# Attention and GLU on one core: VectorE's exponential as one quadratic with two PV products instead of four shifted patterns, and any score job open to either engine

## Chip, cores, metric

The kernel runs on one core of a Trainium2 chip. The metric is device time in microseconds (us) of one execution, medians over several executions. The engines are PE (TensorE; PEld is its weight loads), ACT (ScalarE), DVE (VectorE), POOL (GpSimd) and SP (which issues DMAs).

## The reference, cut to what matters

```python
xn = layernorm(x)                                   # x: 1 x 2048 x 640, bf16
q, k, v = heads(xn @ wqkv)                          # 32 heads of 20
p = softmax(q @ k.T * 20 ** -0.5)                   # 32 x 2048 x 2048: 134 million exponentials
s = merge(p @ v) @ wo
g = silu((sigmoid(xn @ w_gate) * (xn @ w_up)) @ w_down)      # F = 1728
out = x + s * g
```

## The kernel before

Attention is cut into 32 blocks (8 groups of four heads, times 4 chunks of 512 queries). A block has 64 **score jobs**: one head against one tile of 128 keys, a 128x512 tile of scores in one of the program's banks in PSUM (the memory to which it has PE write its products). There are 2,048 jobs in all. PE makes the scores, ACT or DVE makes the exponential, PE multiplies it with V (the **PV** matmuls, four heads at once in four column strips; in the trace before, a round of four starts 0.222 us after the round before it, at the median) into one accumulator bank; the row sums come from a column of ones in V. A clever part of the program is its issue order: at build time a loop with estimated durations decides, step by step, what each engine does next. It fills the gaps of PE with GLU and projection work.

ACT takes two or three jobs at a time, with its own exponential instruction:

```python
exp_act(pt[:, 2, :], bank[nexp % 2])                 # a third job, if there is one: 128x512
exp_act(pt[:, 0:2, :], scA[nexp % 2])                # two jobs at once: 128x1024
```

DVE approximates. It turns scores into integers that are bf16 bits of a power of two, linear between powers; four such patterns, shifted by a quarter octave each (an octave is a factor of two) and weighted through V itself and three scaled copies of it, average the ripple out:

```python
# one per job: float scores in PSUM -> int16
nc.vector.tensor_scalar(out=d["iv"][:, j, :], in0=bank[bk], scalar1=I_OFF, scalar2=I_LOW, op0=ALU.add, op1=ALU.max)
# four per four jobs (128x2048, int16 -> int16), one for each shift k
nc.vector.tensor_scalar(out=pb[:, k, :, :].bitcast(I16), in0=iv, scalar1=0.25, scalar2=cst, op0=ALU.mult, op1=ALU.add)
# four PV matmuls per job
lhsT = vts[...] if not k else vss[pr % 2][:, DKT.index(kt), k - 1, ...]
```

The scaled copies of V exist only for 4 of the 16 key tiles, so DVE takes those tiles whole (four heads each), 512 jobs at most; what it has not taken by the end of a block goes to ACT. The thresholds of the order loop matter later. The one called SLACK below says how soon DVE must be free for a score matmul to be issued for it; the loop reads it at a second place too, where it decides how long a job waiting for conversion may stand back behind a pass:

```python
NPT, NPB, NIV = (2, 4), 2, 2          # buffers: exp outputs (of 2 and of 3 jobs), pass outputs, converted jobs
# ... cut ...
busy = max(0.0, free["DVE"] - now) + T_IV * len(dq)
if d_can and busy <= T_F + T_MODE + PL + SLACK:      # 0.2133 + 0.107 + 0.21 + SLACK
    d_bank = ...                                     # a free PSUM bank for DVE's job
# ... cut: the second place, in DVE's own part of the loop ...
if iv_ok and not (dve_last == "iv" and pass_ok and now < dq[0][3] + SLACK):
```

Of the kernel before, what the change touches and what calls it, by code (L numbers as in the profile page):

```python
# [20 lines left out]
GH = 4  # L21
# [5 lines left out]
ND = 4  # L27
# [4 lines left out]
URGENT, ROUNDS, HOLD, SLACK, LEAD, LAG, D_LAST, D_LAST_END = 0.1, 4, 0.3, 0.1, 20.0, -5.0, 16, 8  # L32
D_ORD, M_ORD, WAIT3, FALL = 0, 1, 0.0, 1

LOG2E = 1.4426950408889634
UNIT = 512.0
ALPHA = (1.0, 215.0 / 256.0, 181.0 / 256.0, 152.0 / 256.0)
NB = len(ALPHA)
I_OFF = 28672.0
I_LOW = -32700.0  # L40


def _log_shift():
    y = (np.arange(4096) + 0.5) / 4096
    tot = np.zeros_like(y)
    for b, a in enumerate(ALPHA):
        z = y + b / NB
        n = np.floor(z)
        tot += a * 2.0 ** n * (1.0 + z - n)
    return -float(np.log2(np.mean(tot / 2.0 ** y)))  # L50


DELTA = _log_shift()
# [3 lines left out]
def kernel(  # L57
# [47 lines left out]
    xnT = persist.tile([P, KD, S], BF16, name="xnT")  # L105
# [3 lines left out]
    vss = [persist.tile([P, max(ND, 1), NB - 1, 2 * GH, VW], BF16, name=f"vs{i}") for i in range(2)] if ND else None  # L109
# [12 lines left out]
    DKT = [(2 * i + 1) * TT // (2 * ND) for i in range(ND)] if ND else []  # L122
    AKT = [k for k in range(TT) if k not in DKT]

    wqkv_v = A_wqkv.rearrange("(kd p) (t c) -> p kd t c", p=P, t=3)
# [20 lines left out]
    def k_mm(ps, g, c):  # L146
        for kd in range(KD):
            nc.tensor.matmul(ps, lhsT=wslice(g, 1, kd), rhs=xnT[:, kd, c * 512:(c + 1) * 512],
                             start=(kd == 0), stop=(kd == KD - 1))
# [21 lines left out]
    def q_mm(ps, g, c):  # L171
        for kd in range(KD):
            nc.tensor.matmul(ps, lhsT=wslice(g, 0, kd), rhs=xnT[:, kd, c * QC:(c + 1) * QC],
                             start=(kd == 0), stop=(kd == KD - 1))
# [12 lines left out]
    def v_mm(ps, w, tts):  # L187
        for i, tt in enumerate(tts):
            for kd in range(KD):
                nc.tensor.matmul(ps[:, i * 2 * GC:(i + 1) * 2 * GC], lhsT=xnT[:, kd, tt * P:(tt + 1) * P],  # L190
                                 rhs=w[:, kd, :], start=(kd == 0), stop=(kd == KD - 1))

    def v_evac(ps, pr, tts, copy=None):
        copy = copy or nc.vector.tensor_copy
        n = len(tts)
        src = ps[:, 0:n * 2 * GC].rearrange("p (t h e) -> p t h e", t=n, e=DH)
        copy(out=vts[pr % 2][:, tts[0]:tts[0] + n, :, 1:1 + DH], in_=src)
        for i, tt in enumerate(tts):
            if tt in DKT:
                vf = wk.tile([P, 2 * GC], FP32, tag="vf", bufs=1, name="vf")  # L200
                copy(out=vf, in_=ps[:, i * 2 * GC:(i + 1) * 2 * GC])
                for b in range(1, NB):
                    nc.gpsimd.tensor_scalar(out=vss[pr % 2][:, DKT.index(tt), b - 1, :, 1:1 + DH],
                                            in0=vf.rearrange("p (h e) -> p h e", e=DH),
                                            scalar1=ALPHA[b], scalar2=0.0, op0=ALU.mult, op1=ALU.add)
# [4 lines left out]
    with tc.tile_pool(name="ln", bufs=2) as lp, \  # L210
# [17 lines left out]
        def constants():  # L228
# [6 lines left out]
            for b in range(1, NB):  # L235
                nc.gpsimd.memset(vss[0][:, :, b - 1, :, 0:1], ALPHA[b])
            nc.gpsimd.memset(vts[0].rearrange("p t h c -> p (t h) c")[:, :, 0:1], 1.0)

        def more_constants():
# [8 lines left out]
            for b in range(1, NB):  # L248
                nc.gpsimd.memset(vss[1][:, :, b - 1, :, 0:1], ALPHA[b])
# [27 lines left out]
        def scale(c):  # L277
# [7 lines left out]
            for kd in range(KD):  # L285
# [4 lines left out]
                dst = xnT[:, kd, c * 512:(c + 1) * 512]  # L290
# [82 lines left out]
    ob = []  # L373
# [6 lines left out]
    T_IV, T_PASS, T_ON = 0.605, 0.605, 0.60  # L380
    NPT, NPB, NIV = (2, 4), 2, 2
# [44 lines left out]
    def k_mm1(ps, g, c, kd):  # L426
        nc.tensor.matmul(ps, lhsT=wslice(g, 1, kd), rhs=xnT[:, kd, c * 512:(c + 1) * 512],
                         start=(kd == 0), stop=(kd == KD - 1))

    def mk_q(b, at):  # L430
# [6 lines left out]
        def mm(kd):  # L437
            nc.tensor.matmul(st["ps"], lhsT=wslice(g, 0, kd), rhs=xnT[:, kd, c * QC:(c + 1) * QC],
# [23 lines left out]
    def u_mm(st, u, i, c, kd):  # L462
        nc.tensor.matmul(st["ps"][0:UC, :], lhsT=wus[u][:, kd, i, :], rhs=xnT[:, kd, c * QC:(c + 1) * QC],  # L463
# [100 lines left out]
    def mk_v(pr, tts, at):  # L564
# [5 lines left out]
        def mm(i, kd):  # L570
            nc.tensor.matmul(st["ps"][:, i * 2 * GC:(i + 1) * 2 * GC],
                             lhsT=xnT[:, kd, tts[i] * P:(tts[i] + 1) * P],
                             rhs=wvs[pr][:, kd, :], start=(kd == 0), stop=(kd == KD - 1))

        def done(t):
            for tt in tts:
                v_at[(pr, tt)] = t + (2.5 if tt in DKT else 0.0)
        nd = sum(tt in DKT for tt in tts)
        return Item([("PE", alloc, [(0.08, lambda i=i, kd=kd: mm(i, kd)) for i in range(len(tts)) for kd in range(KD)]),
                     ("DVE", 0.065 + 0.167 * len(tts) + 0.231 * nd, lambda: v_evac(st["ps"], pr, tts), "free", done)], at)  # L580

    def mk_gu(c, kf, at):
# [16 lines left out]
        def mm(key, i, kd):  # L599
            w = wgu_tiles[(c, k2)]  # L600
            nc.tensor.matmul(st[key][0:fs, :], lhsT=w[:, i, kd, ko * P:ko * P + fs],  # L601
                             rhs=xnT[:, kd, c * QC:(c + 1) * QC], start=(kd == 0), stop=(kd == KD - 1))
# [9 lines left out]
        def mm2(kd):  # L612
            nc.tensor.matmul(st["g"], lhsT=wgu_tiles[(c, k2)][:, 0, kd, P:2 * P],
                             rhs=xnT[:, kd, c * QC:(c + 1) * QC], start=(kd == 0), stop=(kd == KD - 1))
# [83 lines left out]
    def load_out(tt):  # L698
        if tt in out_tiles:
            return  # L700
        if not ob:
            ob.append(late.tile([P, 14 * D], BF16, name="ob", tag="wd"))
        o2 = ob[0][:, tt % 3 * 4 * D:(tt % 3 + 1) * 4 * D]
        out_tiles[tt] = (o2[:, 0:D], o2[:, 2 * D:4 * D].bitcast(FP32), o2[:, D:2 * D])
# [3 lines left out]
    def mk_out(tt, h, at):  # L708
# [21 lines left out]
        def ev():  # L730
            xr, gqr, ot = out_tiles[tt]
            sl = slice(h * HD, (h + 1) * HD)
            tmp = ob[0][:, 12 * D + h * D:13 * D + h * D].bitcast(FP32)
            nc.vector.scalar_tensor_tensor(out=tmp, in0=st["ps"][:, 0:HD], scalar=0.25,
                                           in1=gqr[:, sl], op0=ALU.mult, op1=ALU.mult)
            nc.gpsimd.tensor_tensor(out=ot[:, sl], in0=tmp, in1=xr[:, sl], op=ALU.add)
            if h == 1:
                nc.sync.dma_start(out=out2[tt * P:(tt + 1) * P, :], in_=ot)
        return Item([("PE", alloc, [(0.136, lambda kd=kd: mm(kd)) for kd in range(KD + split)]),
                     ("DVE", 0.40, ev, "free", mark("o", tt, h))], at, need=(NG - 1) * NQC + tt // 4,  # L740
                    pre=[("d", NQC - 1, t4, i) for t4 in range(4) for i in range(2)] + (
# [39 lines left out]
    a_left = {b: [(kt, j) for kt in AKT for j in range(GH)] for b in range(NBLK)}  # L781
    d_left = {b: list(DKT) for b in range(NBLK)}
# [3 lines left out]
    def base():  # L786
        while head_blk[0] < NBLK - 1 and not a_left[head_blk[0]] and not d_left[head_blk[0]]:
# [3 lines left out]
    def claim_act(n):  # L791
        got = []
        for b in range(base(), NBLK):
            while len(got) < n and (a_left[b] or d_left[b]):
                if q_at.get(b, 1e9) > now:
                    return got
                if not a_left[b]:
                    kt = d_left[b].pop()
                    a_left[b] = [(kt, j) for j in range(GH)]
                kt, j = a_left[b].pop(0)  # L800
                if any(x[2] == j for x in got):
                    a_left[b].insert(0, (kt, j))
                    return got
                got.append((b, kt, j))
                claimed[0] += 1
            if len(got) == n:
# [3 lines left out]
    def claim_dve():  # L810
        for b in range(base(), min(NBLK, base() + 2)):
            if d_left[b] and len(a_left[b]) >= (D_LAST if b < NBLK - 1 else D_LAST_END):
                if q_at.get(b, 1e9) > now:
                    return None
                claimed[0] += GH
                return b, d_left[b].pop(0)
# [15 lines left out]
    def add_unit(b, kt, j, src, k, ready, rel):  # L832
        if k is None or k == NB - 1:
# [13 lines left out]
    def pv_emit(us, end):  # L847
        for u in us:
# [7 lines left out]
            if not k:  # L856
                lhsT = vts[pr % 2][:, kt, go * GH + j, 0:DH + 1]
            else:
                lhsT = vss[pr % 2][:, DKT.index(kt), k - 1, go * GH + j, 0:DH + 1]
# [43 lines left out]
    def passes(iv, pb, k):  # L903
        cst = 128.0 * (127.0 + k / NB + DELTA) - I_OFF / 4.0
        nc.vector.tensor_scalar(out=pb[:, k, :, :].bitcast(I16), in0=iv, scalar1=0.25, scalar2=cst,  # L905
                                op0=ALU.mult, op1=ALU.add)


    xfl = xnT.rearrange("p k s -> p (k s)")
# [4 lines left out]
    def tail_load():  # L914
        for t4 in range(4):
            r = slice(4 * (NQC - 1) * P + t4 * P, 4 * (NQC - 1) * P + (t4 + 1) * P)
            o2 = xfl[:, t4 * 4 * D:(t4 + 1) * 4 * D]
            tail.append((o2[:, 0:D], o2[:, 2 * D:4 * D].bitcast(FP32), o2[:, D:2 * D]))
# [3 lines left out]
    def tail_steps():  # L922
# [36 lines left out]
        for t4 in range(4):  # L959
            xr, gqr, ot = tail[t4]  # L960
            nc.vector.scalar_tensor_tensor(out=tmps[t4], in0=mains[t4], scalar=0.25, in1=gqr[:, 0:512],
                                           op0=ALU.mult, op1=ALU.mult)
            if t4 < 2:
                nc.gpsimd.tensor_tensor(out=ot[:, 0:512], in0=tmps[t4], in1=xr[:, 0:512], op=ALU.add)
        xg = xfl[:, 0:16 * D].rearrange("p (t u) -> p t u", u=4 * D)
# [3 lines left out]
                                       in1=xfl[:, 0:16 * D].bitcast(FP32).rearrange(  # L969
                                           "p (t u) -> p t u", u=2 * D)[:, :, D + 512:2 * D],  # L970
                                       op0=ALU.mult, op1=ALU.mult)
        nc.vector.tensor_tensor(out=xg[:, :, D + 512:2 * D], in0=tmp.rearrange("p (t e) -> p t e", e=EX),
                                in1=xg[:, :, 512:D], op=ALU.add)
        for t4 in (2, 3):
            xr, gqr, ot = tail[t4]
            nc.vector.tensor_tensor(out=ot[:, 0:512], in0=tmps[t4], in1=xr[:, 0:512], op=ALU.add)
        for t4 in range(4):
            r = slice(4 * (NQC - 1) * P + t4 * P, 4 * (NQC - 1) * P + (t4 + 1) * P)
            eng = nc.sync if t4 % 2 == 0 else nc.scalar
            eng.dma_start(out=out2[r, :], in_=tail[t4][2])  # L980

    with tc.manual_schedule(engines={ENG.PE, ENG.Activation, ENG.DVE}):
# [32 lines left out]
        def due():  # L1015
            return total * min(1.0, progress() / (NBLK - NQC - 0.2))
# [18 lines left out]
        while pv_block[0] < NBLK or items or glu_items or any(it.i < len(it.ops) for it in active):  # L1035
# [33 lines left out]
            for eng in ("ACT", "DVE"):  # L1069
# [51 lines left out]
                if iv_ok and not (dve_last == "iv" and pass_ok and now < dq[0][3] + SLACK):  # L1121
                    dve_last = "iv"
                    d, j, bk, _ = dq.pop(0)
                    nc.vector.tensor_scalar(out=d["iv"][:, j, :], in0=bank[bk], scalar1=I_OFF,  # L1124
                                            scalar2=I_LOW, op0=ALU.add, op1=ALU.max)
# [4 lines left out]
                    if d["n"] == GH:  # L1130
                        dve_pass.append(d)
                elif pass_ok:
# [3 lines left out]
                    if k == 0:  # L1136
                        d["pb"] = w2.tile([P, NB, GH, QC], BF16, tag="pb", bufs=NPB, name="pb")
# [170 lines left out]
```

## Time and profile before

Time: 879.36 us (878.77 to 879.71, 3 runs). The profiled execution has a span of 879.2 us.

| stage | us |
|---|---|
| start: layer norm, first projections | 0 to 43 |
| main stage: first to last exp of ACT | 43.0 to 856.8 |
| tail: last normalisation, output product | 856.8 to 879.2 |

The head of the profile page: busy time, share of the span and instructions of each engine, then the granted clock of TensorE (the part of its full speed that the chip let it run at) in 40 equal slices, in tenths, then the chain of work that ended last by engine.

```profile
PE 822.0 (93%) x7176; PEld 297.1 (34%) x7176; DVE 708.5 (81%) x1203; ACT 829.9 (94%) x1098; POOL 100.3 (11%) x142
...
PEclk9999999999999999999999999999999999989999
...
ACT 42%; PE 35%; DVE 13%; issue 8%; DMA 1%; POOL 1%; POOLq 0%; DVEq 0%; ACTq 0%
```

Three stretches of the main stage from the table of stretches (from:to, length, then busy us of each engine with its instruction count, clock, DMA share, GB/s):

```profile
200.00:300.00 100.00, 97.51 (x851) 35.46 (x849) 82.25 (x140) 98.27 (x128) 7.98 (x9) 1.00 0.23 59
300.00:400.00 100.00, 97.23 (x871) 35.22 (x871) 79.28 (x132) 99.50 (x133) 9.15 (x13) 1.00 0.25 68
400.00:500.00 100.00, 98.33 (x870) 33.60 (x867) 92.81 (x157) 99.06 (x126) 6.99 (x7) 1.00 0.21 56
```

ACT has nothing left; DVE has 18, 21 and 7 of 100 us free here. Records of one engine overlap (the next instruction starts before the record of the last one ends), so for costs I use the distance from one start to the next. Here are ACT and then DVE from the timeline (start, duration, engine, what):

```profile
404.39 1.06 ACT L87 ACTIVATE pt_5530<-scA_570 128x1024 bf16<-128x1024 f32 x1
405.29 1.07 ACT L87 ACTIVATE pt_5540<-scA_571 128x1024 bf16<-128x1024 f32 x1
406.20 1.08 ACT L87 ACTIVATE pt_5550<-scA_570 128x1024 bf16<-128x1024 f32 x1
407.10 0.67 ACT L87 ACTIVATE pt_5561<-bk_573 128x512 bf16<-128x512 f32 x1
407.58 1.11 ACT L87 ACTIVATE pt_5561<-scA_571 128x1024 bf16<-128x1024 f32 x1
```

```profile
404.48 0.69 DVE L1124 TENSOR_SCALAR iv<-bk_574 128x512 int16<-128x512 f32 x1
405.08 0.69 DVE L905 TENSOR_SCALAR pb<-iv 128x2048 int16<-128x2048 int16 x1
405.68 0.69 DVE L1124 TENSOR_SCALAR iv<-bk_573 128x512 int16<-128x512 f32 x1
```

A two-job exp occupies ACT for 0.90 us although its record says 1.06 to 1.08 (404.39 to 405.29); a one-job exp 0.48 (407.10 to 407.58). Over the main stage the medians are 0.904 and 0.477. A conversion and a pass occupy DVE 0.60 each. And the groups of instructions (count | busy us, mean ns | idle before them, what ended it):

```profile
L905 DVE TENSOR_SCALAR pb<-iv 128x2048 int16<-128x2048 int16 x412 | 287.9, 723 | 2.7
L1124 DVE TENSOR_SCALAR iv<-bk_574 128x512 int16<-128x512 f32 x147 | 100.6, 685 | 37.9 <-PE bk_574 L820 37.2
L1124 DVE TENSOR_SCALAR iv<-bk_573 128x512 int16<-128x512 f32 x147 | 100.4, 683 | 31.6 <-PE bk_573 L820 31.4
...
L1124 DVE TENSOR_SCALAR iv<-bk_572 128x512 int16<-128x512 f32 x118 | 80.6, 683 | 20.0 <-PE bk_572 L820 19.5
```

Conversions are 147 + 147 + 118 = 412, so DVE did 412 jobs (20%) and ACT 1,636. DVE idled 89 us before conversions, nearly all of it waiting for PE's score matmuls.

### The profile page before, as it was taken

To read this page: it belongs to the slowest core of one execution; us is meant where nothing else is said; L and a number is where in the kernel's file an instruction comes from. 1 tells how busy PE (TensorE), PEld (TensorE's weight loads), DVE (VectorE), ACT (ScalarE), POOL (GpSimd) and SP (SyncE) were. 2 spreads that over 40 slices of the span, in tenths; PEclk is the share of its full clock that TensorE was granted. 3 is DMA by queue.
4 is the path that set the end of the run, shared out by engine and by line. 5 is a ranking of instruction groups with operands and counts; after the bars stand their busy time and mean duration, and the time that the engine had idled before them with its cause. 6 is when DMAs were issued, how large, how long until landed. Compare 5 with 4: busy or idle time off the path is not lost.

```text
span 879.2 us, 18755 instructions
## 1 busy us (share of the span) xinstructions
PE 822.0 (93%) x7176; PEld 297.1 (34%) x7176; DVE 708.5 (81%) x1203; ACT 829.9 (94%) x1098; POOL 100.3 (11%) x142
## 2 busy tenths in 40 slices
PE   2799999999999999999999999999999999987896
PEld 1532333333333333343333333333323333322333
DVE  6568878986789987769999878688688698678984
ACT  4699999999999999999999999999999999999990
POOL 5200000112000000111000000012000000001333
PEclk9999999999999999999999999999999999989999
DMA  7241222222112232211123233211122221321432
GB/s 207 61 123 44 62 63 77 62 55 53 49 52 78 72 81 73 71 44 35 37 57 94 64 74 82 62 45 41 52 73 70 60 61 49 109 82 47 116 111 83
DMA packets 92987, 62.32 MB, mean 71 GB/s; under 512 B 34649, under 2 KB 86409, under 8 KB 92897
## 3 DMA queue, kind: packets, MB, share of 16 engines
q1 hardware_dynamic: 91456, 59.48, 24.9%
q10 hardware_dynamic: 1440, 1.64, 0.6%
q8 instruction: 56, 0.92, 0.5%
q14 instruction: 35, 0.28, 0.1%
HBM read 46.24 MB, written 12.39 MB: 67 GB/s over the span
## 4 chain that ended last, share of the span: by engine, by line
ACT 42%; PE 35%; DVE 13%; issue 8%; DMA 1%; POOL 1%; POOLq 0%; DVEq 0%; ACTq 0%
PE oacc L860 9%; DVE pb L905 5%; PE scA_571 L820 5%; PE scA_570 L820 5%; DVE iv L1124 4%; PE bk_574 L601 4%; ACT tnh L87 2%; PE bk_572 L463 1%; PE bk_574 L639 1%; PE bk_574 L463 1%; PE bk_572 L601 1%; DVE xn L283 1%; PE bk_573 L601 1%; PE bk_573 L639 1%; DMA xt<-in_A_x_dram 1%
## 5 line engine op out<-in xcount | busy, mean ns | idle before, releaser
L905 DVE TENSOR_SCALAR pb<-iv 128x2048 int16<-128x2048 int16 x412 | 287.9, 723 | 2.7
L1124 DVE TENSOR_SCALAR iv<-bk_574 128x512 int16<-128x512 f32 x147 | 100.6, 685 | 37.9 <-PE bk_574 L820 37.2
L1124 DVE TENSOR_SCALAR iv<-bk_573 128x512 int16<-128x512 f32 x147 | 100.4, 683 | 31.6 <-PE bk_573 L820 31.4
L890 POOL TENSOR_TENSOR on_bf<-on,rl 128x512 bf16<-128x512 f32 x30 | 40.9, 1364 | 583.7 <-DMA rl<-rd 390.0
L1124 DVE TENSOR_SCALAR iv<-bk_572 128x512 int16<-128x512 f32 x118 | 80.6, 683 | 20.0 <-PE bk_572 L820 19.5
L601 PE MATMUL bk_574<-xnT,wgu 128*128 128x512 bf16 x305 | 84.0, 383 | 0.1
L820 PEld LDWEIGHTS <-kT_81 32*128 32x128 bf16 x1024 | 39.0, 91 | 127.8 <-issue 124.5
L820 PEld LDWEIGHTS <-kT_82 32*128 32x128 bf16 x1024 | 41.5, 91 | 118.7 <-issue 109.3
L860 PE MATMUL oacc<-pb,vs_86 128*21 128x512 bf16 x648 | 76.4, 383 | 2.8 <-DVE pb L905 2.4
L860 PE MATMUL oacc<-pb,vs_85 128*21 128x512 bf16 x588 | 71.0, 381 | 0.0
L601 PEld LDWEIGHTS <-wgu 128*128 128x128 bf16 x520 | 40.2, 98 | 64.4 <-issue 38.4
L639 PEld LDWEIGHTS <-hT 128*128 128x128 bf16 x448 | 36.0, 97 | 43.4 <-issue 33.0
L860 PEld LDWEIGHTS <-v_84 128*21 128x21 bf16 x1024 | 31.2, 91 | 48.9 <-issue 39.1
L860 PEld LDWEIGHTS <-v_83 128*21 128x21 bf16 x1024 | 30.4, 91 | 44.8 <-issue 35.8
L639 PE MATMUL bk_574<-wd,hT 128*128 128x320 bf16 x238 | 44.7, 302 | 0.2 <-DVE iv L1124 0.2
L609 DVE SCALAR_TENSOR_TENSOR hT<-tnh,bk_574 128x512 bf16<-128x512 bf16 x34 | 23.2, 684 | 15.4 <-PE bk_574 L601 14.5
L860 PE MATMUL oacc<-pb,v_84 128*21 128x512 bf16 x216 | 32.0, 386 | 0.6 <-DVE on L873 0.5
L601 PE MATMUL bk_573<-xnT,wgu 128*128 128x512 bf16 x110 | 31.0, 383 | 0.3 <-DVE iv L1124 0.3
L860 PEld LDWEIGHTS <-vs_86 128*21 128x21 bf16 x648 | 21.8, 91 | 23.1 <-issue 15.3
L601 PE MATMUL bk_572<-xnT,wgu 128*128 128x512 bf16 x105 | 29.4, 382 | 0.1
L860 PE MATMUL oacc<-pb,v_83 128*21 128x512 bf16 x196 | 29.2, 382 | 0.0
L820 PE MATMUL scA_570<-q_96,kT_82 32*128 32x512 bf16 x124 | 25.3, 390 | 2.7 <-ACT pt_10608 L87 1.0
(1863 smaller groups left out, 2386.3 us busy)
## 6 DMA issues: line engine op xcount, KB each, us to landing
wgu<-in_B_w_gate_dram SPq DMA_DIRECT2D x24, 320.0 KB
wgu<-in_B_w_up_dram SPq DMA_DIRECT2D x24, 320.0 KB
rl<-rd SPq DMA_DIRECT2D x120, 64.0 KB
gq_dram<-gqs SPq DMA_DIRECT2D x32, 160.0 KB
ob<-gq_dram SPq DMA_DIRECT2D x12, 320.0 KB
wd<-in_B_w_down_dram SPq DMA_DIRECT2D x1, 2080.0 KB
oU<-on_bf SPq DMA_DIRECT2D x104, 20.0 KB
ob<-in_A_x_dram SPq DMA_DIRECT2D x12, 160.0 KB
```

The source lines that it names most:

```text
L87: return nc.scalar.add_instruction(mybir.InstActivation(func=func, name=nc.get_next_instruction_name(), engine=ENG.Activation, ins=[nc.sca ...
L283: nc.vector.tensor_scalar(out=xn[:, i, :], in0=xts[c][:, i, :], scalar1=rstds[c][:, i, :], scalar2=nb[:, i, :], op0=ALU.mult, op1=ALU.add)
L463: nc.tensor.matmul(st["ps"][0:UC, :], lhsT=wus[u][:, kd, i, :], rhs=xnT[:, kd, c * QC:(c + 1) * QC], start=(kd == 0), stop=(kd == KD - 1))
L601: nc.tensor.matmul(st[key][0:fs, :], lhsT=w[:, i, kd, ko * P:ko * P + fs], rhs=xnT[:, kd, c * QC:(c + 1) * QC], start=(kd == 0), stop=(kd ...
L609: nc.vector.scalar_tensor_tensor(out=hT[0:fs, kf, :], in0=st["t"][0:fs, :], scalar=1.0, in1=st["u"][0:fs, :], op0=ALU.add, op1=ALU.mult)
L639: nc.tensor.matmul(st["ps"][:, 0:HD], lhsT=hT[0:fsz[kf], kf, t4 * P:(t4 + 1) * P], rhs=wd[0:fsz[kf], kf, h * HD:(h + 1) * HD], start=(kf = ...
L820: nc.tensor.matmul(dst, lhsT=kTs[(b // NQC) % 2][32 * j:32 * j + 32, kt * P:(kt + 1) * P], rhs=qts[b % 3][32 * j:32 * j + 32, :], start=Tr ...
L860: nc.tensor.matmul(oacc[32 * j:32 * j + DH + 1, :], lhsT=lhsT, rhs=u["src"], start=first, stop=last, tile_position=(0, 32 * j), skip_group ...
L890: nc.gpsimd.tensor_tensor(out=on_bf, in0=on, in1=rl, op=ALU.mult)
L905: nc.vector.tensor_scalar(out=pb[:, k, :, :].bitcast(I16), in0=iv, scalar1=0.25, scalar2=cst, op0=ALU.mult, op1=ALU.add)
L1124: nc.vector.tensor_scalar(out=d["iv"][:, j, :], in0=bank[bk], scalar1=I_OFF, scalar2=I_LOW, op0=ALU.add, op1=ALU.max)
```

## The change

Its intent: make DVE's share of the exponentials cheaper for PE and freer to place. The integers are now exact bf16 bits in 1/128 octave. Write a score's power as 2^E (1 + f). One pass keeps the exponent, 2^E (1 + 1/128); one makes (1 + f)/2 from the fraction; a multiply gives 2^E (1 + f)^2/2. Their sum is a quadratic that follows 2^f within 0.2% (0.13% rms, computed), up to a constant that is folded into the offset. The two parts need only two PV matmuls, with the same V; so no scaled copies, and no reserved tiles: any job may go to either engine, one at a time, and DVE's job is now picked before ACT's and no longer after them. The freed memory goes to deeper buffers, and thresholds are retuned.

```diff
-URGENT, ROUNDS, HOLD, SLACK, LEAD, LAG, D_LAST, D_LAST_END = 0.1, 4, 0.3, 0.1, 20.0, -5.0, 16, 8
+URGENT, ROUNDS, HOLD, SLACK, LEAD, LAG, D_LAST, D_LAST_END = 0.05, 3, 0.2, 0.6, 40.0, 0.0, 24, 16
+... M_END = 1.5                                  # other work is spread to 1.5 blocks from the end, was 4.2
+NPT, NPB, NIV = (3, 7), 3, 3
-    T_IV, T_PASS, T_ON = 0.605, 0.605, 0.60
-    NPT, NPB, NIV = (2, 4), 2, 2
+    T_PASS = (0.605, 0.605, 1.15)
@@ V: the scaled copies go (vf, vss and their POOL work) @@
@@ claims @@
-    a_left = {b: [(kt, j) for kt in AKT for j in range(GH)] for b in range(NBLK)}
-    d_left = {b: list(DKT) for b in range(NBLK)}
+    left = {b: [list(range(TT)) for _ in range(GH)] for b in range(NBLK)}
@@ cut: ACT takes from the front of the head with most left, DVE from the back, and DVE picks first @@
@@ PV: one V for all @@
-            if not k:
-                lhsT = vts[pr % 2][:, kt, go * GH + j, 0:DH + 1]
-            else:
-                lhsT = vss[pr % 2][:, DKT.index(kt), k - 1, go * GH + j, 0:DH + 1]
+            lhsT = vts[pr % 2][:, kt, go * GH + j, 0:DH + 1]
@@ passes @@
-        nc.vector.tensor_scalar(out=pb[:, k, :, :].bitcast(I16), in0=iv, scalar1=0.25, scalar2=cst,
-                                op0=ALU.mult, op1=ALU.add)
+        if k == 0:
+            nc.vector.tensor_scalar(out=pb[:, 0, :, :].bitcast(I16), in0=iv, scalar1=0x7F80, scalar2=1,
+                                    op0=ALU.bitwise_and, op1=ALU.bitwise_or)
+        elif k == 1:
+            nc.vector.tensor_scalar(out=pb[:, 1, :, :].bitcast(I16), in0=iv, scalar1=0x007F, scalar2=0x3F00,
+                                    op0=ALU.bitwise_and, op1=ALU.bitwise_or)
+        else:
+            nc.vector.tensor_tensor(out=pb[:, 1, :, :], in0=iv.bitcast(BF16), in1=pb[:, 1, :, :], op=ALU.mult)
@@ cut: layout of xnT by chunks, buffers of the output stage moved into xnT and wd @@
```

## The prediction

> **What bounds it now.** The table of stretches gives ACT 98 to 100% busy in every stretch from 42 to 856 us, DVE 79 to 93%, PE 86 to 98%. PE's busy time is modelled, so I take start-to-start times from the instructions in order of time. ACT: 689 two-bank exps every 0.904 us, 256 one-bank exps every 0.477 us, plus 41 us of tanh and abs; in all about 796 of those 814 us, so ACT is the bound, and its exps cost 0.462 us per score job (128x512; 1,636 of 2,048 jobs are ACT's). DVE does the other 412 jobs (20%): an integer conversion every 0.60 us for one job, and four passes every 0.60 us for four jobs (groups: 412 conversions, 412 passes), 1.20 us per job. With 144 us of other work DVE is occupied only about 649 of 814 us. Its idle time stands before conversions: 88 us waiting for PE's score matmuls (list of waits). PE cannot feed it sooner, because each DVE job costs four PV matmuls: 412 x 4 + 1,636 = 3,284, or 821 rounds of four at 0.213 us, 175 us[...].
>
> **What the change does.**
> - DVE per four jobs: four conversions (2.40), two bitwise passes (0.60 each, as today's int16 passes), one bf16 multiply of two tensors. [...] Sum 4.74 against 4.80 us: DVE work per job does not change (1.19).
> - PE: two PV matmuls per DVE job in place of four: 824 fewer, 206 rounds, 44 us at the same share.
> - The scaled copies of V go (DVE 3 us; POOL 22 us, off the chain).
> - Any job may go to DVE, one at a time and from any key tile, instead of four heads of four reserved key tiles (a cap of 512 jobs); buffers are deeper (exp outputs 2 and 4 to 3 and 7, pass outputs 2 to 3); GLU work is spread to nearer the end.
>
> **On the critical path.** Neither PE's 44 us nor DVE's 3 us counts by itself: ACT is saturated. The gain is ACT jobs moved to DVE, 0.462 us each, once PE feeds DVE promptly. With DVE = 142 + 1.22x us and the main stage = 814 - 0.462(x - 412) us: DVE 90% occupied gives x = 465 and 789 us; 95% gives x = 489 and 778; full would give x = 512 and 768. I take 92 to 93%, x about 475, main stage about 785 us. Start (42 us) and tail (24 us) stay.
>
> **Prediction: 850 us** (-3.3%), range 838 to 866; faster by over 2%: 0.82, within 2%: 0.13, slower: 0.05.
>
> **What would show it.** Conversions rise from 412 to 455-495; PV matmuls fall from 3,284 to about 2,520; ACT stays 97% or more busy and its exps fall by 50 to 80 jobs; DVE occupied 90% or more, wait before conversions well below 88 us; bitwise passes every 0.60 us[...]; PE less busy.
>
> **What would make it wrong.** [...] Free PSUM banks instead of PE time limiting how often DVE is fed: DVE stays near 80% and the gain is under 2%. POOL and DVE blocking each other more (passes of up to 1.77 us exist today). Or the end of the last blocks, where GLU and output work now land, leaving ACT idle.

The sum of 4.74 us per four jobs: 2.40 for the conversions, 1.20 for the two passes, the rest for the multiply, a figure that nothing in the kernel before supports. From 4.74 come the 1.19 us per job, the statement that DVE's work per job does not change, and through it x, about 475 jobs, and the 850 us. Measured afterwards: 2.40 + 0.609 + 0.599 + 1.133 = 4.74. The 0.213 us for a round of four PV matmuls is the program's own T_PV; with the 0.222 of the trace the 206 rounds are 46 us in place of 44.

## The result, and the profile after

Time: 846.54 us (845.62 to 848.07, 4 runs) against 879.54 us for the kernel before in the same rounds: ratio 0.9621, 95% interval 0.9594 to 0.9648. Here and below a ratio is the mean time of one kernel's fast runs over that of the other's fast runs of the same rounds, so it is not quite the ratio of the medians quoted. The profiled execution has a span of 843.7 us. All outputs are right.

Head of the page, as before: busy times, clock, chain by engine.

```profile
PE 789.0 (94%) x6371; PEld 276.5 (33%) x6427; DVE 778.9 (92%) x1220; ACT 792.8 (94%) x978; POOL 78.4 (9%) x88
...
PEclk9999999999999999999999999999999999999998
...
PE 40%; DVE 28%; ACT 24%; issue 5%; DMA 2%; POOL 1%; SPq 0%; POOLq 0%; DVEq 0%; ACTq 0%
```

The same three stretches:

```profile
200.00:300.00 100.00, 96.94 (x803) 33.17 (x807) 98.28 (x152) 98.35 (x119) 6.28 (x4) 1.00 0.22 60
300.00:400.00 100.00, 95.56 (x808) 33.24 (x813) 95.94 (x144) 98.55 (x121) 5.35 (x4) 1.00 0.25 66
400.00:500.00 100.00, 95.64 (x757) 31.64 (x762) 97.65 (x150) 98.27 (x118) 5.09 (x4) 1.00 0.20 58
```

ACT is as full as it was (98%), DVE went from 82, 79 and 93 of 100 us to 98, 96 and 98, PE a little down. The chain that ended last no longer runs mostly through ACT: DVE's part went from 13 to 28% and ACT's from 42 to 24%. Groups of DVE:

```profile
L889 DVE TENSOR_TENSOR pb<-iv,pb 128x2048 bf16<-128x2048 bf16 x122 | 152.1, 1246 | 0.8
L1107 DVE TENSOR_SCALAR iv<-bk_545 128x512 int16<-128x512 f32 x188 | 128.0, 681 | 7.6 <-PE bk_545 L798 7.4
L1107 DVE TENSOR_SCALAR iv<-bk_544 128x512 int16<-128x512 f32 x156 | 106.3, 681 | 5.9 <-PE bk_544 L798 5.6
...
L1107 DVE TENSOR_SCALAR iv<-bk_546 128x512 int16<-128x512 f32 x143 | 97.3, 681 | 10.4 <-PE bk_546 L798 9.8
L883 DVE TENSOR_SCALAR pb<-iv 128x2048 int16<-128x2048 int16 x122 | 89.0, 729 | 2.4
...
L886 DVE TENSOR_SCALAR pb<-iv 128x2048 int16<-128x2048 int16 x122 | 87.0, 713 | 0.0
```

Conversions are 188 + 156 + 143 = 487, 75 more than before, and the idle time before them fell from 89 to 24 us. The timeline of DVE shows the new passes and the multiply, and that of POOL (last line) one instruction:

```profile
402.74 0.68 DVE L886 TENSOR_SCALAR pb<-iv 128x2048 int16<-128x2048 int16 x1
403.33 0.68 DVE L1107 TENSOR_SCALAR iv<-bk_544 128x512 int16<-128x512 f32 x1
403.93 1.21 DVE L889 TENSOR_TENSOR pb<-iv,pb 128x2048 bf16<-128x2048 bf16 x1
405.06 0.68 DVE L1107 TENSOR_SCALAR iv<-bk_545 128x512 int16<-128x512 f32 x1
...
409.06 2.05 DVE L889 TENSOR_TENSOR pb<-iv,pb 128x2048 bf16<-128x2048 bf16 x1
411.03 0.68 DVE L1107 TENSOR_SCALAR iv<-bk_546 128x512 int16<-128x512 f32 x1
...
408.76 1.27 POOL L865 TENSOR_TENSOR on_bf<-on,rl 128x512 bf16<-128x512 f32 x1 [26.87 <-DMA rl<-rd]
```

A bitwise pass of 2,048 elements occupies DVE 0.59 to 0.60 us (402.74 to 403.33), like the arithmetic pass before, and the multiply 1.13 us (403.93 to 405.06). The multiply at 409.06 took 2.05 us; POOL had started its product on_bf<-on,rl at 408.76. The whole kernel has 19 such stretched passes (over 0.9 us, multiplies over 1.4 us), all of them overlapping a POOL instruction, 13 us in all; another 19 overlap one and are not stretched, so overlap alone is not enough. In the kernel before, 23 passes were stretched, by 14 us, again all of them overlapping a POOL instruction. This cost did not change. Why some overlaps stretch a pass and others do not is not shown.

To follow the time through all runs I use one sum. ACT's **work** is 0.904 us times its two-job exps, plus 0.477 times its one-job exps, plus 41 us of tanh and abs (the start-to-start distances read above). The main stage is this work plus a **rest**: ACT waiting, and starts that come later than the minimum.

| | DVE's jobs | two-job, one-job exps | ACT work | rest | main stage |
|---|---|---|---|---|---|
| before | 412 | 690, 256 | 786.9 | 26.9 | 813.7 |
| after | 487 | 731, 99 | 749.0 | 30.5 | 779.6 |

The span fell by 35.4 us. ACT's work fell by 37.9, the rest rose by 3.6; the start is 2.9 shorter (first exp at 43.0, now 40.1) and the tail 1.7 longer. So the gain is ACT's work, and it comes to 0.50 us for each of the 75 jobs moved: 0.46 for a job (before: 745.9 us of exps over 1,636 jobs), and the remainder because fewer of ACT's exps are of a single job: a job costs 0.452 us in a pair and 0.477 alone.

That ACT's work fell is read from the trace. Why DVE's share could rise, whether the smaller PV work was needed at all, and what each part of the change gave, is not. Hence the experiments.

### The profile page after: what moved, and what is told of

It is laid out like the page before. It is cut to its first block, busy times and chain, and to the rows that moved or that the text cites. A ratio compares the mean times of both kernels' runs of the same rounds, so it can differ in the third digit from the quotient of the medians.

```text
span 843.7 us, 16982 instructions
## 1 busy us (share of the span) xinstructions
PE 789.0 (94%) x6371; PEld 276.5 (33%) x6427; DVE 778.9 (92%) x1220; ACT 792.8 (94%) x978; POOL 78.4 (9%) x88
## 3 DMA queue, kind: packets, MB, share of 16 engines
q1 hardware_dynamic: 91456, 59.48, 25.1%
## 4 chain that ended last, share of the span: by engine, by line
PE 40%; DVE 28%; ACT 24%; issue 5%; DMA 2%; POOL 1%; SPq 0%; POOLq 0%; DVEq 0%; ACTq 0%
DVE iv L1107 10%; PE oacc L835 8%; PE scA_543 L798 6%; PE scA_542 L798 6%; DVE pb L889 5%; PE bk_546 L580 4%; DVE pb L886 3%; DVE pb L883 3%; PE bk_544 L580 2%; PE bk_546 L443 1%; PE bk_545 L580 1%; PE bk_546 L618 1%; DVE hT L588 1%; PE bk_544 L618 1%; ACT tnh L80 1%
## 5 line engine op out<-in xcount | busy, mean ns | idle before, releaser
L889 DVE TENSOR_TENSOR pb<-iv,pb 128x2048 bf16<-128x2048 bf16 x122 | 152.1, 1246 | 0.8
L1107 DVE TENSOR_SCALAR iv<-bk_545 128x512 int16<-128x512 f32 x188 | 128.0, 681 | 7.6 <-PE bk_545 L798 7.4
L1107 DVE TENSOR_SCALAR iv<-bk_544 128x512 int16<-128x512 f32 x156 | 106.3, 681 | 5.9 <-PE bk_544 L798 5.6
L1107 DVE TENSOR_SCALAR iv<-bk_546 128x512 int16<-128x512 f32 x143 | 97.3, 681 | 10.4 <-PE bk_546 L798 9.8
L883 DVE TENSOR_SCALAR pb<-iv 128x2048 int16<-128x2048 int16 x122 | 89.0, 729 | 2.4
L798 PEld LDWEIGHTS <-kT_81 32*128 32x128 bf16 x1024 | 40.9, 91 | 143.0 <-issue 141.0
L886 DVE TENSOR_SCALAR pb<-iv 128x2048 int16<-128x2048 int16 x122 | 87.0, 713 | 0.0
L580 PE MATMUL bk_546<-xnT,wgu 128*128 128x512 bf16 x283 | 82.4, 382 | 3.4 <-DVE iv L1107 1.3
L798 PEld LDWEIGHTS <-kT_82 32*128 32x128 bf16 x1024 | 45.1, 91 | 120.7 <-issue 109.2
L835 PE MATMUL oacc<-pb,v_84 128*21 128x512 bf16 x512 | 77.0, 382 | 2.3 <-DVE pb L889 1.6
L835 PE MATMUL oacc<-pb,v_83 128*21 128x512 bf16 x462 | 72.7, 382 | 0.8 <-DVE pb L883 0.4
L835 PEld LDWEIGHTS <-v_84 128*21 128x21 bf16 x1280 | 25.6, 90 | 49.8 <-issue 40.6
L835 PEld LDWEIGHTS <-v_83 128*21 128x21 bf16 x1255 | 25.6, 90 | 49.7 <-issue 40.3
L618 PE MATMUL bk_544<-wd,hT 128*128 128x320 bf16 (+1 forms) x182 | 35.3, 303 | 0.0
L618 PE MATMUL bk_546<-wd,hT 128*128 128x320 bf16 (+1 forms) x168 | 32.4, 302 | 0.3 <-DVE iv L1107 0.3
L580 PE MATMUL bk_544<-xnT,wgu 128*128 128x512 bf16 x99 | 30.3, 383 | 0.8
L798 PE MATMUL scA_542<-q_94,kT_82 32*128 32x512 bf16 x137 | 27.2, 383 | 2.2 <-ACT pt_9623 L80 0.9
L798 PE MATMUL scA_542<-q_93,kT_81 32*128 32x512 bf16 x138 | 27.9, 384 | 1.3 <-DVE q_93 L177 0.8
L798 PE MATMUL scA_543<-q_94,kT_82 32*128 32x512 bf16 x136 | 27.5, 383 | 1.1 <-ACT pt_7894 L80 0.6
```

The source lines that it names most:

```text
L580: nc.tensor.matmul(st[key][0:fs, :], lhsT=w[:, i, kd, ko * P:ko * P + fs], rhs=xnT[:, c, kd, :], start=(kd == 0), stop=(kd == KD - 1))
L618: nc.tensor.matmul(st["ps"][:, 0:HD], lhsT=hT[0:fsz[kf], kf, t4 * P:(t4 + 1) * P], rhs=wd[0:fsz[kf], kf, h * HD:(h + 1) * HD], start=(kf = ...
L798: nc.tensor.matmul(dst, lhsT=kTs[(b // NQC) % 2][32 * j:32 * j + 32, kt * P:(kt + 1) * P], rhs=qts[b % 3][32 * j:32 * j + 32, :], start=Tr ...
L835: nc.tensor.matmul(oacc[32 * j:32 * j + DH + 1, :], lhsT=lhsT, rhs=u["src"], start=first, stop=last, tile_position=(0, 32 * j), skip_group ...
L883: nc.vector.tensor_scalar(out=pb[:, 0, :, :].bitcast(I16), in0=iv, scalar1=0x7F80, scalar2=1, op0=ALU.bitwise_and, op1=ALU.bitwise_or)
L886: nc.vector.tensor_scalar(out=pb[:, 1, :, :].bitcast(I16), in0=iv, scalar1=0x007F, scalar2=0x3F00, op0=ALU.bitwise_and, op1=ALU.bitwise_or)
```

## Experiments

The theories at the start. **A**: DVE was short of work because PE, loaded with four PV matmuls per DVE job, could not feed it; halving them raises the share (my prediction). **B**: free placement, deeper buffers and thresholds raised the share; the quadratic was needed only to allow them. **C**: time follows PE's load or the buffers directly and not the jobs moved. The expectations use the letters more loosely: in those of e6 and e7, Theory A is the other half of my prediction, that the time is ACT's load. Later letters are S (the threshold SLACK), R (free placement), Bf (buffers) and D (free PSUM banks, not DVE's time, set the share).

Which engine gets which job is fixed by the order loop when the program is built. So DVE's job counts below are decisions of the loop, not something that the chip did; for e3, e10 and e11 the count was known when the expectation was written, and only the time was a forecast. Each kernel was timed in rounds with the kernel before, which had medians of 879.5, 879.6 and 880.5 us in the three sets.

### e6_cap13: everything new, but DVE held to its old share

```diff
+    d_took = {b: 0 for b in range(NBLK)}
+    D_CAP = 13
-            if n_left[b] >= (D_LAST if b < NBLK - 1 else D_LAST_END):
+            if d_took[b] < D_CAP and n_left[b] >= (D_LAST if b < NBLK - 1 else D_LAST_END):
+                d_took[b] += 1
```

> The new kernel with DVE held to 13 of the 64 score jobs of each block, 416 in all against 412 before and 487 now. Everything else is new, PE's relief too. Theory A (the time is ACT's load, so the whole gain is the jobs moved, 0.46 us each): 71 jobs x 0.46 = 33 us back, 874 to 882 us, ACT still 97% or more busy, DVE and PE visibly idle. Rival C (PE's 44 us or the deeper buffers shorten the time by themselves): 850 to 865 us.

Measured: 880.62 us, ratio to before 1.0014 (0.9986 to 1.0042). DVE took 412 jobs, exactly as before. ACT's work is 784.6 us, the rest 33.1. With all of PE's relief, deeper buffers and free placement, but without the moved jobs, there is no gain at all. (TensorE's clock was at half rate for 58 us near the end, more on which in the last section; but the rest is only 2.6 us above the new kernel's, so that this cannot hide a gain of 33.) C is out; the gain is the moved jobs.

### e1_pv_twice: PE's old PV load in the new kernel

Each part of a DVE job is multiplied with V twice; the exponent offset is lowered by one octave, so that the result stays right. M_END is 2.0, since with 1.5 the order loop came to its end without placing the last loads.

```diff
-    return 128.0 * (127.0 - float(np.log2(k)))
+    return 128.0 * (126.0 - float(np.log2(k)))
-                        pb_left.append([2 * len(d["jobs"]), 0.0])
+                        pb_left.append([4 * len(d["jobs"]), 0.0])
+                            add_unit(b, kt, j, d["pb"][:, k // 2, x, :], 0, end + EL, d["rel"])
                             add_unit(b, kt, j, d["pb"][:, k // 2, x, :], k, end + EL, d["rel"])
```

> The new kernel, but every PV matmul of a DVE job is issued twice (the exponent is lowered by one, so the result stays right), and M_END is 2.0 in place of 1.5 because the order generator found no place for the last loads at 1.5. DVE's cost per job is unchanged; PE again has four PV matmuls per DVE job. Theory A (PE's halved PV work is what lets DVE be fed more often): the share falls back, conversions 400 to 435, DVE idle before conversions returns to over 60 us, time 868 to 885 us. Theory B (free choice of jobs, deeper buffers and retuned thresholds brought the gain): conversions stay above 470 and the time below 855 us.

Measured: 881.24 us, ratio 1.0018 (0.9996 to 1.0041). The time is the one that A expected and the share the one that B expected, so each theory failed on the other count: DVE still took 487 jobs. PE had 3,509 PV matmuls, and now ACT waits: the rest is 61.2 us, against 30.5 in the new kernel and 42.1 in its control with the same M_END (e0, below, in a run some 4 us above its median). From its list of waits (who waited for whom: us, times, longest), the waits of exps, and below them the same of e0:

```profile
ACT pt L80 <- PE bk L798: 23.9, 41, 1.8
...
ACT pt L80 <- PE scA L798: 5.9, 14, 1.2
...
ACT pt L80 <- PE oacc L835: 3.2, 3, 1.3
```

```profile
ACT pt L80 <- PE bk L798: 11.8, 19, 1.8
ACT pt L80 <- PE scA L798: 8.1, 10, 4.2
```

Summed over all exps, the idle time in front of them is 35.9 us here against 22.3 in e0, 11.8 in the new kernel and 9.5 before: ACT waits, for score matmuls above all.

So, in the new kernel, the halved PV work is needed: with twice as much of it PE no longer keeps ACT fed at the larger share. It does not set the share.

### e0_mend2: control for M_END

Two kernels needed M_END 2.0. This is the new kernel with that alone.

```diff
-D_ORD, M_ORD, WAIT3, FALL, M_END = 0, 1, 0.0, 1, 1.5
+D_ORD, M_ORD, WAIT3, FALL, M_END = 0, 1, 0.0, 1, 2.0
```

> Control: the new kernel with M_END 2.0 in place of 1.5, as two of the other runs needed it. Expected within 0.5% of the new kernel, 842 to 851 us.

Measured: 851.85 us (848.14 to 856.26), ratio 0.9670 (0.9630 to 0.9710), 489 jobs. Just outside what I expected. This kernel scatters more than the others and its interval overlaps that of the new kernel (0.9594 to 0.9648), so the 5 us between the medians may or may not be M_END's. Against this control the doubled PV work costs 3.5% by the ratios (1.0018 against 0.9670), some 30 us.

### e2_quad_alone: the quadratic and nothing else

The kernel before with the new passes, the two PV matmuls and one V; reserved tiles, buffers and thresholds stay. (Edit: the hunks "V", "PV" and "passes" of the change, with the offset and the estimated durations that belong to the passes.)

> The kernel before with the quadratic alone (two bitwise passes, one multiply, two PV matmuls, same V); reserved key tiles, buffer counts and thresholds stay those of before. Theory A: conversions 465 to 500 and 848 to 858 us, most of the gain. Theory B: conversions under 435 and over 868 us.

Measured: 885.19 us, ratio 1.0068 (1.0037 to 1.0099): no gain, rather a small loss. DVE took 408 jobs. PE was relieved of 828 PV matmuls (2,456 in place of 3,284), and yet DVE's wait for PE before conversions grew from 88 to 111.5 us:

```profile
DVE iv L1106 <- PE bk L800: 111.5, 109, 3.2
```

This is what A cannot explain. PE had time: its last GLU matmul ended at 698.9 us, in the kernel before at 765.4. The issue order put GLU work forward and sent DVE no more jobs. (TensorE's clock was at half rate for 89 us near the end, see the last section; but most of the longer wait is older than that: up to 700 us, at the full clock, the wait for PE before conversions is 80 us against 63.)

### e8_slack01 and e9_quad_slack: one threshold

With SLACK 0.1 a job is issued for DVE only if DVE will be free within 0.63 us. The multiply lasts 1.13 us. My reading: if PE's turn to fill ACT's banks (the only time at which it also makes a DVE job) falls inside a multiply, DVE gets none until the next turn. e8 puts SLACK 0.1 back into the new kernel; e9 puts SLACK 0.6 into the quadratic alone.

```diff
 e8, on the kernel after
-URGENT, ROUNDS, HOLD, SLACK, ... = 0.05, 3, 0.2, 0.6, ...
+URGENT, ROUNDS, HOLD, SLACK, ... = 0.05, 3, 0.2, 0.1, ...
 e9, on e2
-URGENT, ROUNDS, HOLD, SLACK, ... = 0.1, 4, 0.3, 0.1, ...
+URGENT, ROUNDS, HOLD, SLACK, ... = 0.1, 4, 0.3, 0.6, ...
```

> The new kernel with one threshold put back, SLACK 0.6 to 0.1: a score matmul is issued for DVE only when DVE will be free within 0.63 us, not 1.13. The quadratic alone left the share at 408 of 2,048 jobs, so something else in the change raised it to 487. Theory S (the 1.13 us multiply outlasts the old limit, so a fill that falls inside a multiply sends DVE nothing): conversions fall to 400 to 440 and the time rises to 865 to 882 us, DVE's wait for PE before conversions over 60 us. Theory R (the free choice of jobs) and theory Bf (deeper buffers): share stays above 470, time below 855 us.

Measured: 865.65 us, ratio 0.9839 (0.9811 to 0.9867), 442 jobs, and DVE waits 67.4 us for PE before conversions. One number costs 45 of the 75 moved jobs and 19 of the 33 us. The share is two jobs above the range that I gave Theory S, the time at its lower end. SLACK stands at two places of the loop and this run changes both; which of them counts, no run separates.

> The kernel before with the quadratic and SLACK 0.6, nothing else new. Theory S: conversions rise from 408 to over 450 and the time falls to 850 to 865 us. Theories R and Bf: share stays within 400 to 430, time 875 to 890 us.

Measured: 871.39 us, ratio 0.9905 (0.9883 to 0.9927), 436 jobs. Better than the quadratic alone by 28 jobs and 14 us, but a miss for S as the only cause: it fell between the two ranges. Something else is missing beside SLACK.

### e3_old_params: all thresholds back

```diff
-URGENT, ROUNDS, ..., D_LAST_END = 0.05, 3, 0.2, 0.6, 40.0, 0.0, 24, 16      and M_END = 1.5
+URGENT, ROUNDS, ..., D_LAST_END = 0.1, 4, 0.3, 0.1, 20.0, -5.0, 16, 8       and M_END = 4.2
```

> The new kernel with all thresholds of before (SLACK 0.1 among them, M_END 4.2); 444 conversions in the built program, 43 fewer than in the new kernel. Theory: 0.46 us per job, 866 us; 858 to 872 us, the same as with SLACK alone put back (865.7), so that SLACK is the threshold that counts. If the others counted too, over 874 us.

Measured: 862.06 us, ratio 0.9795 (0.9763 to 0.9826), 444 jobs. That is no slower than SLACK alone put back, so SLACK is the threshold that counts.

### e5_reserved and e4_old_buffers: free placement, and depth of buffers

e5 gives DVE whole reserved key tiles again (4 of 16, the old claim rule), with M_END 2.0. e4 has the old buffer counts.

```diff
 e5: claim_dve, in place of the free choice
+        if not had:
+            for b in range(base(), min(NBLK, base() + 2)):
+                if d_left[b] and len(a_left[b]) >= (D_LAST if b < NBLK - 1 else D_LAST_END):
+                    kt = d_left[b].pop(0)
+                    d_set[:] = [(b, kt, j) for j in range(GH)]
+                    break
+        return d_set.pop(0) if d_set else None
 e4
-NPT, NPB, NIV = (3, 7), 3, 3
+NPT, NPB, NIV = (2, 4), 2, 2
```

> The new kernel with DVE's jobs again taken as whole reserved key tiles (four of sixteen, four heads each); thresholds and buffers stay new (M_END 2.0 for 1.5, as the generator needs). Theory R: conversions 400 to 440 and 865 to 885 us. Theories S and Bf: above 465 and below 858 us. The cap of reserved tiles is 512.

Measured: 852.36 us, ratio 0.9697 (0.9677 to 0.9717), 488 jobs. Its control with the same M_END has 0.9670 (0.9630 to 0.9710): the intervals overlap, so nothing that can be told is lost. Free placement, the change's most visible freedom, gave nothing by itself once the buffers were deep. (DVE still picks its job before ACT here, as in the new kernel.)

> The new kernel with the buffer counts of before: exp outputs (2, 4) for (3, 7), pass outputs 2 for 3, converted jobs 2 for 3. Theory Bf: conversions 400 to 440 and 865 to 885 us. Theories S and R: above 465 and below 858 us.

Measured: 863.76 us, ratio 0.9813 (0.9791 to 0.9836), 485 jobs. The share stays, as S and R said, but their time (below 858 us) is missed, and it is 17 us worse than the new kernel's: the rest is 46.6 in place of 30.5 us, and the idle time before exps 23.6 in place of 11.8. Shallow buffers do not keep jobs from DVE here; they leave ACT waiting. (All the counts went back together; which one it is, I did not test.)

### e11_quad_retuned and e10_retuned_before: what is missing without buffers, or without the quadratic

```diff
 e11 on e2, e10 on the kernel before
-URGENT, ROUNDS, ..., D_LAST_END = 0.1, 4, 0.3, 0.1, 20.0, -5.0, 16, 8
+URGENT, ROUNDS, ..., D_LAST_END = 0.05, 3, 0.2, 0.6, 40.0, 0.0, 24, 16
-            return total * min(1.0, progress() / (NBLK - NQC - 0.2))
+            return total * min(1.0, progress() / (NBLK - 1.5))
```

> The kernel before with the quadratic and all the new thresholds; reserved tiles and old buffers stay. The built program has 428 conversions, 16 more than before, so by ACT's load alone 872 us. If thresholds were all that was missing beside the quadratic it would come to 846 to 855; with reserved tiles and shallow buffers both in place I expect 866 to 882 us.

Measured: 880.87 us, ratio 1.0001 (0.9971 to 1.0031), 428 jobs, and no gain. The other new thresholds cost something here: e9, with SLACK alone, had 436 jobs and 871.4 us, and the intervals are apart. What e11 lacks against the new kernel is free placement, depth and the new order of picking (DVE before ACT). Free placement is missing in e5 (488 jobs) and depth in e4 (485 jobs), and the share came in both; but both have the new order of picking, which no run takes away alone. So what holds e11 at 428 is not shown: it may be that order, or the reserved tiles and the shallow buffers together.

> The kernel before with the new thresholds (SLACK 0.6 and the rest, M_END 1.5), but still four shifted patterns, reserved tiles and old buffers. The built program has 444 conversions. Theory T (retuning alone would have done it): 860 to 868 us, 0.46 us less for each of the 32 jobs moved. Theory A' (without the halved PV work PE cannot keep up and ACT waits for it, as when PV was issued twice): 872 to 890 us, ACT's idle time larger than before.

Measured: 883.38 us, ratio 1.0022 (0.9999 to 1.0046). DVE took 444 jobs and ACT's work fell by 16 us, but the rest rose from 26.9 to 48.1 and the idle time before exps from 9.5 to 26.1: ACT waits for PE, as Theory A' said. Retuning alone is worth nothing. But that the four PV matmuls per job (3,380 in all) are the reason is not shown by this run: e11, which is this kernel with the quadratic and so two per job, is no faster that can be told (1.0001, 0.9971 to 1.0031), and e4, with two per job and the same shallow buffers, has 23.6 us of idle time before exps, nearly as much. The buffers and the other thresholds are rivals here; the case for the smaller PV work rests on e1 against e0. One thing more: the share rose by 32 jobs in a kernel without the multiply, so looser thresholds feed DVE more also where no long instruction stands in the way, and my reading of e8 is at most a part of the truth.

### e7_two_lines: a cheaper pair of parts

If DVE's time now limits its share, a cheaper exponential should move more jobs. The converted bits, read as bf16, are already a linear pattern. I use them as the first part and the same bits plus 64 (half an octave) as the second: one conversion and a quarter of one 0.60 us pass per job, 0.75 us in place of 1.19, and still two PV matmuls with the same V. The second pattern weighs 1.41 times the first, so the ripple does not cancel fully: 0.53% rms, 1.5% at most, computed, against 0.13% of the quadratic.

```diff
-    T_PASS = (0.605, 0.605, 1.15)
+    T_PASS = 0.605
-NPT, NPB, NIV = (3, 7), 3, 3
+NPT, NPB, NIV = (3, 7), 3, 5
+        nc.vector.tensor_scalar(out=d["pb"][:, 0:n, :].bitcast(I16), in0=d["iv"][:, 0:n, :], scalar1=64.0, scalar2=None,
+                                op0=ALU.add)
+                    add_unit(*d["jobs"][j], d["iv"][:, j, :].bitcast(BF16), 0, end + EL, (iv_left, d["i"]))
@@ cut: the three passes go; the offset is refitted; iv is freed by its last PV matmul @@
```

> The new kernel with a cheaper approximation on DVE: the converted bits used directly as bf16 and once more with 64 added (half an octave), no scaled V, so one conversion and a quarter of one pass per job, 0.75 us in place of 1.19, and still two PV matmuls per job. Ripple 0.53% rms in place of 0.13%, computed. Theory A (balance of ACT and DVE): by ACT and DVE alone 640 to 680 conversions and about 770 us; PE cannot follow that far, so I expect PE to become the bound, conversions 520 to 600 and 805 to 835 us. Rival D (PSUM banks, not DVE's time, set how many jobs DVE gets now): conversions stay within 475 to 505 and the time within 838 to 852 us with DVE idle.

Measured: 818.3 us, ratio 0.9302 (0.9284 to 0.9320) to the kernel before, faster than both. 543 jobs, ACT's work 724.6 us, rest 25.1. D is out: with cheaper work on DVE the share rose. (The edit also takes NIV from 3 to 5, and with the multiply it takes away DVE's longest instruction, on which my reading of e8 turns; so cost per job and length of instruction are not separated.) Busy times and DVE's wait:

```profile
PE 764.2 (94%) x6428; PEld 273.0 (34%) x6483; DVE 626.7 (77%) x1046; ACT 766.2 (94%) x968; POOL 73.3 (9%) x88
```

```profile
DVE iv L1101 <- PE bk L799: 102.4, 197, 1.9
```

DVE is again idle before conversions (102 us, 88 in the kernel before) while ACT and PE are full. So this variant is limited by what PE and the issue order deliver; that PE's time and not the order is its bound was not tested.

### All runs in one table

| kernel | DVE's jobs | ACT work | rest | time, us | ratio |
|---|---|---|---|---|---|
| before | 412 | 786.9 | 26.9 | 879.4 | |
| e2 quadratic alone | 408 | 788.5 | 33.2 | 885.2 | 1.007 |
| e10 thresholds alone | 444 | 770.7 | 48.1 | 883.4 | 1.002 |
| e11 quadratic + thresholds | 428 | 778.0 | 40.2 | 880.9 | 1.000 |
| e9 quadratic + SLACK | 436 | 774.2 | 31.0 | 871.4 | 0.991 |
| e6 new, DVE capped | 412 | 784.6 | 33.1 | 880.6 | 1.001 |
| e1 new, PV doubled | 487 | 749.6 | 61.2 | 881.2 | 1.002 |
| e8 new, SLACK 0.1 | 442 | 772.3 | 29.7 | 865.7 | 0.984 |
| e4 new, old buffers | 485 | 751.1 | 46.6 | 863.8 | 0.981 |
| e3 new, old thresholds | 444 | 771.7 | 24.5 | 862.1 | 0.980 |
| e5 new, reserved tiles | 488 | 748.3 | 37.7 | 852.4 | 0.970 |
| e0 new, M_END 2.0 | 489 | 748.1 | 42.1 | 851.9 | 0.967 |
| after | 487 | 749.0 | 30.5 | 846.5 | 0.962 |
| e7 two linear parts | 543 | 724.6 | 25.1 | 818.3 | 0.930 |

(Work and rest are of the profiled execution; that of e0 was its slowest, 856.3 us, so its rest is some 4 us too high for its median.)

## Why the prediction was right, and where its reasoning failed

- **The time and the sum.** 850 us (838 to 866) predicted, 846.5 measured. Main stage 785 predicted, 780 measured; 475 jobs predicted, 487 measured; 2,520 PV matmuls predicted, 2,535 measured; DVE 92 to 93% occupied predicted, and by start-to-start distances about 723 of 780 us, 93%, measured. (ACT's "about 796" us in the prediction is a slip of addition: its terms give 786, so that the rest was 28 us and not 18. Nothing later in it uses the 796.)
- **ACT as the bound.** Right, and now shown: e6 has everything but the moved jobs and gains nothing.
- **Costs on DVE.** Right. For the bitwise passes the prediction took the 0.60 us of the arithmetic passes of the kernel before; they came every 0.60 to 0.61 us. That a bitwise form would run as fast was assumed and shown only by the trace after. The multiply's time was the author's estimate, which nothing in the kernel before showed; it came every 1.13 us, and the sum of 4.74 us per four jobs holds.
- **The mis-sized term.** The main stage came out 5 us shorter than predicted. Twelve more jobs moved than expected give 5.5 us; a moved job was priced 0.462 us and brought 0.50, because ACT's one-job exps also fell from 256 to 99, another 3; and the rest, which the prediction kept, grew by 3.6.
- **The step that failed.** "PE cannot feed it sooner, because each DVE job costs four PV matmuls", and then "once PE feeds DVE promptly". I read 88 us of DVE waiting for PE as PE having no time. The runs show that it was in good part the issue order declining to send work. Relieving PE alone left the share at 408 and the wait at 111 us, and PE did its GLU work sooner (e2); loading PE again left the share at 487 (e1). What raised the share was SLACK (45 of 75 jobs, e8; 28 of them also without the rest of the change, e9 against e2), and beside it something that e11 lacks and that is not singled out: free placement, depth or the new order of picking. The PV relief was needed for another reason: without it the larger share makes ACT wait for PE (e1 against e0, some 30 us).
- **Luck.** The prediction does not mention SLACK or the order of picking. It took for granted that DVE would be fed promptly once PE was relieved; for 45 of the 75 jobs that is owed to SLACK, and with the old SLACK the new kernel has 442 jobs, below the 455 to 495 that the prediction asked for. Given that feeding, its estimate of how full DVE would get was right by its own reasoning; that the feeding came was in good part luck.
- **Free placement** was listed as a part of the gain. By itself, with deep buffers, it gave nothing (e5 against e0).
- **POOL** did not hold DVE up more: 19 stretched passes and 13 us, against 23 and 14.

What stays open: how SLACK acts within a fill was argued from the durations and the rule, and shown only by the count of jobs, and which of its two places counts; what beside SLACK raised the share; why ACT waits in e10; which of the buffer counts matters; and what bounds e7.

## What to carry to other kernels

When one engine is full and another has idle time, price the change by the work that will move, then ask who decides that it moves; here a threshold in the issue order had to be raised, or the smaller PV work alone brought nothing. A wait "for PE" in a profile says that PE's instruction came late, not that PE had no time: relieve the named engine alone once, before believing it. Parts of a change can each be worth nothing and together 4%, so undo them from the full version as well as adding them to the old one.

## What the traces show of DVE's costs and of TensorE's clock

- Bitwise_and then bitwise_or on 128x2048 int16 ran every 0.609 and 0.599 us (medians of the two passes), as the multiply and add on the same shape did, 0.602 in the kernel before.
- The lengths of the records are not the costs: at the median the record of the 2,048-element multiply is 1,215 ns long, and those of the two bitwise passes 693 and 683; the engine takes its next instruction 1.133, 0.609 and 0.599 us after the start, and that is what to budget with.
- The clock records of the kernels before and after have two values, 1.0 and 0.5 of full speed. In the kernels e2, e11 and e6 (mean granted clock 0.948, 0.957 and 0.964) the clock was at half rate for 89, 72 and 58 us near the end; in e2 and e6 this came after the last full-size GLU matmuls, while PE went on with score and PV matmuls of 32x128 and 128x21 tiles. In e2 the last GLU matmul ended at 698.9 us and half rate began at 706.4, and between 706.4 and 747 us, at half rate, PE was busy for 35.63 of 40.60 us. Three stretches of e2 and one of the kernel before (the clock is the third figure from the end):

```profile
690.00:699.00 9.00, 8.76 (x71) 3.56 (x68) 8.94 (x15) 9.00 (x14) 0.00 (x0) 1.00 0.37 104
699.00:706.40 7.40, 4.42 (x51) 1.51 (x50) 3.18 (x6) 7.40 (x12) 1.26 (x1) 1.00 0.41 120
706.40:747.00 40.60, 35.63 (x230) 7.33 (x229) 29.82 (x44) 37.85 (x51) 2.29 (x1) 0.50 0.20 60
```

```profile
776.40:800.00 23.60, 16.82 (x172) 5.31 (x168) 17.36 (x28) 23.47 (x33) 1.45 (x2) 1.00 0.08 22
```

  In the new kernel the GLU work lasts until 793.8 us, and half rate in the main stage is down to nothing: its clock record stays at 1.0 from 23.2 us until 839.0, where that of the kernel before is at 0.5 from 769.6 to 776.4. What decides is not shown. The kind of matmul alone does not: the last line is of score and PV matmuls only, at the full clock. PE's busy share did fall just before half rate began in e2 (8.76 of 9.00 us, then 4.42 of 7.40), but no run isolates it, nor what the half rate costs.
